# A gated linear attention followed by a two-layer network, on one core: second copy of v made by ScalarE in the first block, h copied out of PSUM by ScalarE for four turns, k' and the first states by VectorE, and the stages set at other slots

## The chip, the cores and the metric

The program runs on one core of a Trainium2 chip. The core has five engines that run their own instruction queues in order: TensorE (PE, with its weight loads shown apart as PEld), VectorE (DVE), ScalarE (ACT), GpSimd (POOL) and SyncE (SP), which here only issues DMA transfers. An engine that waits for another holds up everything behind the waiting instruction in its own queue. The metric is the device time of one execution in microseconds (us); lower is better.

## The reference

The first half is a recurrence over time for each of 4 x 8 heads of dimension 48, over 768 steps; the second half is a two-layer network on its output.

```python
f = 1.0 / (1.0 + np.exp(-f_logit))                       # q, k, v, f_logit: (4, 8, 768, 48)
for t in range(S):
    state = f[:, :, t, :, None] * state + np.einsum('bhd,bhe->bhde', k[:, :, t], v[:, :, t])
    y[:, :, t] = np.einsum('bhd,bhde->bhe', q[:, :, t], state)
x = y.transpose(0, 2, 1, 3).reshape(3072, 384)
h = x @ w_in                                             # (384, 2048)
sp = np.maximum(h, 0.0) + np.log1p(np.exp(-np.abs(h)))
out = (h * erf(sp)) @ w_out                              # (2048, 384)
```

All inputs and the output are float32, except that the weights come as 64-bit numbers, which the kernel rounds on the chip.

## The kernel before, in words

**Tiles.** Time is cut into 24 chunks g of 128 steps (six per batch entry), three chunks to a block of 384 rows; there are eight blocks. Within a chunk the decay is undone: q' is q times the cumulated decay, k' is k divided by it, so that the chunk's output is a masked product of scores and v, plus q' times the state that the chunks before have left.

**Stages of a chunk.** stage_d (L348): TensorE sums the logarithms of the decays (ps_d), ScalarE takes two exponentials (dp, kd), VectorE makes q' (qd, L372) and an engine makes k' (kd, L376): VectorE in block 0, GpSimd in all others. stage_t (L380): TensorE transposes both (ps_t), ScalarE copies q' out (qA, L395), ScalarE or VectorE copies k' out (kT, L397, L399). stage_s (L418): TensorE makes the state increments dS and the scores sc; VectorE masks the scores (L460) and next_state (L403) adds the increment to the old state (L415, VectorE) and multiplies by the chunk's total decay (L416, GpSimd). stage_y (L468): TensorE multiplies, in one go, masked scores and q' in qA with v and the state, which share the tile sv (L489), and ScalarE copies the result to xT (L493). From block 3 on stage_y of one chunk and stage_s of the next are one stage.

**The second copy of v.** A chunk's v is loaded twice: once as vt (for the state increments), and once, by load_sv (L222) in four 48 KB transfers, into sv beside the state. There are two sv tiles, which take turns. In each of the four transfers 64 steps of four heads go to one half of the partitions; these are rows that vt also holds, on the same or the other half.

**The network.** hidden (L544) makes h of a block in four groups of 512 columns. A group is two units u; a unit is six matmuls (L556) into a PSUM tile of two banks, which is then copied to the tile Hg: by ScalarE for blocks 0 and 1 (L566), by VectorE for the others (L568). There are two such PSUM tiles (ps_moe), which the output product (ops, L589, in project) also uses, so the unit after next waits for the copy. Each group is activated by `activate` (L503): a sigmoid (L156) into e, three tanh terms x (L159) that VectorE multiplies into e (L164), a last tanh (L524) and the product with h (L526). There are two e tiles, so the sigmoid of a group waits until L526 of the group before the last is done. A call of act_step moves the running groups on by one step each.

**The order.** The scheduler is off; instructions stand on their engines in the order in which the code issues them. First block 0's attention is written out (L705 to L744), with the loading and rounding of w_in between. Then the loop at L763 runs through turns `it`: turn it makes h of block it, the attention of block it + 1 and, from the third turn on (it = 2), the output of block it - 2. Each turn is a row of slots, one matmul of hidden or project each (96 in a full turn). At a slot may stand: a stage of attention (the list `at`, L770), an act_step (the rules at L788 to L797), loads, the preparation of the decays of block it + 2 (`prepare`, L330: a clamp on VectorE, Exp and Ln on ScalarE), and a step of weight rounding, which is one ScalarE and six VectorE instructions for each of 16 pieces of the weights (round_piece, L268).

**What ScalarE changes tables for.** Exp and Ln need one table, Sigmoid and Tanh another; each change is an ACT_TABLE_LOAD.

Of the kernel before, what the change touches and what calls it, by code (L numbers as in the profile page):

```python
# [45 lines left out]
ALU = mybir.AluOpType  # L46
# [27 lines left out]
def kernel(  # L74
# [10 lines left out]
    nc = tc.nc  # L85
    B, H, S, D = q.shape
# [8 lines left out]
    C = P // 2  # L95
    NCH = S // P
    CPB = 3
    TB = CPB * P
    n_blocks = B * S // TB
# [9 lines left out]
    def fixed(name, shape, dtype=FP32, pool=const):  # L109
        return pool.tile(shape, dtype, name=name)  # L110
# [14 lines left out]
    def rows(r, n=D):  # L125
        return slice(DP * r, DP * r + n)
# [53 lines left out]
    NV, NQ, NG = 3, 3, 10  # L180
    ADJACENT = 3
    vts = [fixed(f"vt{i}", [P, d_model], pool=fix) for i in range(NV)]

    NS, PAD = 2, DP - D
    svs = [fixed(f"sv{i}", [P, 2, 2, HP, D + 2 * PAD], pool=fix) for i in range(NS)]
# [33 lines left out]
    def half(c):  # L219
        return slice(C * c, C * (c + 1))  # L220

    def load_sv(g, queue=None):  # L222
        b, n = divmod(g, NCH)
        for r in range(2):
            for c in range(2):
                t0 = n * P + c * C
                (queue or nc.sync).dma_start(
                    out=svs[g % NS][half(1 - r), r, c, :, PAD : PAD + D],
                    in_=v[b, r::2, t0 : t0 + C, :].rearrange("a t d -> t a d"),
                )  # L230


    PIECE = 768
# [96 lines left out]
    def prepare(blk, j0, j1):  # L330

        lt = lts[blk][:, j0:j1, :].rearrange("t j c -> t (j c)")
        nc.vector.tensor_scalar(
            out=lt, in0=lt, scalar1=LOGIT_MIN, scalar2=None, op0=ALU.max
        )
        use_exp_ln()
        nc.scalar.activation(out=lt, in_=lt, func=AF.Exp, scale=-1.0)
        nc.scalar.activation(out=lt, in_=lt, func=AF.Ln, bias=1.0)
# [9 lines left out]
    def stage_d(g):  # L348
        blk, j = divmod(g, CPB)
        if blk == 0:  # L350
            both = ps_moe.tile([P, 2, 512], FP32, name="ps_d0", tag="moe")
            ps, totals[g] = both[:, 0, 0:d_model], both[:, 1, 0 : 2 * HP]
            busy.append(both[:, 1, P : 2 * P])
        else:
            ps = ps_at.tile([P, 512], FP32, name="ps_d", tag="at")[:, 0:d_model]
        nc.tensor.matmul(ps, lhsT=tri[:], rhs=lts[blk][:, j, :], start=True, stop=True)  # L356
        use_exp_ln()
        dp = dps[g % 2]
        kd = kds[g % 2][:, :, 0:D]
        nc.scalar.activation(  # L360
            out=dp[:, :, 0:D], in_=ps.rearrange("t (h d) -> t h d", d=D), func=AF.Exp, scale=-1.0
        )
        nc.scalar.activation(out=kd, in_=ps.rearrange("t (h d) -> t h d", d=D), func=AF.Exp)
        if blk > 0:
            for c in range(2):
                end = C * (c + 1)
                for a in range(HP):
                    nc.sync.dma_start(
                        out=Tall[:, g, c, a : a + 1],
                        in_=dp[end - 1 : end, 2 * a : 2 * a + 2, :].rearrange("o r d -> o (r d)"),  # L370
                    )
        nc.vector.tensor_tensor(  # L372
            out=qd[:, :, 0:D], in0=qns[g % NQ][:].rearrange("t (h d) -> t h d", d=D),
            in1=dp[:, :, 0:D], op=ALU.mult,
        )
        (nc.vector if blk == 0 else nc.gpsimd).tensor_tensor(  # L376
            out=kd, in0=kns[g % NQ][:].rearrange("t (h d) -> t h d", d=D), in1=kd, op=ALU.mult
        )

# [23 lines left out]
    def next_state(k, dS):  # L403

        g, c = divmod(k, 2)
        g1, c1 = divmod(k + 1, 2)
        for r in range(2):
            old = svs[g % NS][rows(r), r, c, :, PAD : PAD + D]
            new = svs[g1 % NS][rows(r), r, c1, :, PAD : PAD + D]
            total = Tall[rows(r), g, c, :].unsqueeze(2).broadcast_to((D, HP, D))  # L410
            add = dS[rows(r), c, :].rearrange("p (a d) -> p a d", a=HP)
            if k % (2 * NCH) == 0:
                nc.vector.tensor_tensor(out=new, in0=add, in1=total, op=ALU.mult)
                continue
            nc.vector.tensor_tensor(out=new, in0=add, in1=old, op=ALU.add)  # L415
            nc.gpsimd.tensor_tensor(out=new, in0=new, in1=total, op=ALU.mult)  # L416

    def stage_s(g):  # L418
        b, n = divmod(g, NCH)
# [124 lines left out]
    def hidden(blk, gi):  # L544

        own = n_made[0] % NG
        gr = {"h": Hgs[own], "done": False}
        n_made[0] += 1
        groups[blk, gi] = gr
        for u in range(FG // 2):  # L550
            hps = ps_moe.tile([P, 2, 512], FP32, name="hps", tag="moe")
            for j in range(2):
                ft = gi * FG + 2 * u + j
                assert ft * n_pieces // n_ft in rounded
                for kt in range(n_k):
                    nc.tensor.matmul(  # L556
                        hps[:, j, 0:TB],
                        lhsT=w_in_sb[:, kt, ft * P : (ft + 1) * P],
                        rhs=xTs[blk][:, kt, :],
                        start=(kt == 0), stop=(kt == n_k - 1),  # L560
                    )
                    if j == 1 and kt == n_k - 1:
                        assert all(i in rounded for i, x in enumerate(HOMES) if x == own)
                        to = gr["h"][:, 2 * u : 2 * u + 2, :]
                        if blk < 2:
                            nc.scalar.copy(out=to, in_=hps[:, :, 0:TB])  # L566
                        else:
                            nc.vector.tensor_copy(out=to, in_=hps[:, :, 0:TB])  # L568
                        if u == FG // 2 - 1:
                            acts.append(activate(gr))  # L570
                    yield
# [37 lines left out]
    def slots(it):  # L609

        if it >= n_blocks:
            return project(it - 2)
        made = [hidden(it, gi) for gi in range(n_g)]
        return chain(*made) if it < 2 else chain(*made[:2], project(it - 2), *made[2:])
# [20 lines left out]
    with tc.manual_schedule():  # L635
# [7 lines left out]
        load_f(1)  # L643
        load(1, "qk")
        load_f(2)
        load_sv(0)
        load_piece(0)
        load(1, "v")
        load(2)
        load_sv(1)  # L650
        load_piece(1)
        load_piece(2)
        for g in range(CPB, 2 * CPB):
# [3 lines left out]
            out=tri[:], in_=tri[:], pattern=[[1, P]], compare_op=ALU.is_ge, fill=0.0,  # L657
# [43 lines left out]
        def weights_steps(n):  # L701
            for _ in range(n):
                weights_step()
# [10 lines left out]
        load_piece(3)  # L714
        stage_d(1)
        prepare(0, 2, 3)
        stage_s(0)
        weights_steps(2)
        stage_t(1)
        load(4, "qk")  # L720
        load_piece(4)
        stage_d(2)
        weights_steps(2)
        stage_y(0)
        load_sv(2)
# [37 lines left out]
        for it in range(n_blocks + 2):  # L763
            blk = it + 1
            if it + 2 < n_blocks:
                for j in range(CPB):
                    load_f((it + 2) * CPB + j)
            todo = deque(stages(blk) if blk < n_blocks else [])
            n = n_slots[it]
            at = [int(3 + (n - 13) / max(1, len(todo)) * i) for i in range(len(todo))]  # L770
            for s, _ in enumerate(slots(it)):
                due += 1 if it == 0 and s < 36 else 0.75
                while due >= 1:
                    weights_step()
                    due -= 1
                if s % 6 == 3:
                    load_more()
                if at and s == at[0]:
                    at.pop(0)
                    f, g = todo.popleft()  # L780
                    f(g)
                    if f in (stage_y, stage_y_s):
                        if g + NS < n_chunks:
                            load_sv(g + NS)
                        load_to(g + LOOK)
                if it + 2 < n_blocks and s == (16 if it < 2 else 30):
                    prepare(it + 2, 0, CPB)
                if it == 0:  # L788
                    step = s >= 16 and s % 8 == 4
                elif it == 1:  # L790
                    step = s % 8 == 4
                elif it == 2:
                    step = s % 3 == 1
                elif it < n_blocks:
                    step = s % 7 in (2, 5)
                else:
                    step = s % 3 == 2  # L797
                if step and not 66 <= s < 72:
                    act_step()
                if it == n_blocks - 1 and s in (5, 40):  # L800
                    next(check)
            assert not todo
# [214 lines left out]
```

## Time and profile before

| | |
|---|---|
| time, median of 3 runs | 664.28 us (663.15 to 665.3) |
| span of the profiled execution | 663.1 us |
| TensorE busy | 618.4 us (93%) |
| VectorE busy | 454.3 us (69%) |
| ScalarE busy | 416.7 us (63%) |
| GpSimd busy | 92.1 us (14%) |
| mean TensorE clock granted | 0.965 |
| moved by DMA | 41.83 MB |

A line of the profile names a line of the program, an engine and an operation, then the tile written and the tiles read with their shape, how often, busy time, mean duration of one in ns, and after a bar the idle time of the engine just before it with the instruction that ended the idle time (the releaser). In a timeline the first two numbers are start and duration in us, and the brackets hold the idle time before. TensorE works on float32 in two passes, so that a matmul of the code is two instructions of the trace: a full unit of six matmuls is 12 of them. The end of a matmul is modelled, and a DMA counts as landed when its last part has.

### The profile page before, as it was taken

Reading aid. Unit: us, or ns where it says so; the run is one execution under the profiler, and the core shown is the slowest. Engines: PE = TensorE matmul, PEld = TensorE weight load, DVE = VectorE, ACT = ScalarE, POOL = GpSimd, SP = SyncE. Lnnn points to the kernel's source line nnn. Section 1 sums busy time; section 2 is a strip of 40 time slices with the busy share of each in tenths; the row PEclk is TensorE's granted clock in tenths of the full one; section 3 lists DMA queues with packets and bytes.
Section 4 is the critical chain, followed back from the end, with each engine's and each line's share of the span. In section 5 each row is a group of like instructions: output and inputs, shape, how many; then the busy total and the mean of one; then the engine's idle time right before and its main releaser. Section 6 shows DMA issues by size and latency. Waiting matters only on the chain.

```text
span 663.1 us, 11920 instructions
## 1 busy us (share of the span) xinstructions
PE 618.4 (93%) x4871; PEld 384.3 (58%) x4871; DVE 454.3 (69%) x525; ACT 416.7 (63%) x405; POOL 92.1 (14%) x120
## 2 busy tenths in 40 slices
PE   7749799796987999999999999999999999999996
PEld 6735466463554656666666656666666555555553
DVE  5667899989758387676767577676766578268450
ACT  5315775583796756696778866875657547266440
POOL 1212211221222001120112101120121100000000
PEclk9759999899799999999999999999999999999999
DMA  9796569342022141225022132032000100000101
GB/s 190 183 238 154 145 168 250 57 74 53 0 49 49 42 79 16 34 49 121 0 50 48 49 73 47 8 76 51 1 13 1 37 1 0 10 27 0 37 1 39
DMA packets 158909, 41.83 MB, mean 63 GB/s; under 512 B 150656, under 2 KB 153728, under 8 KB 158848
## 3 DMA queue, kind: packets, MB, share of 16 engines
q1 hardware_dynamic: 156768, 40.61, 28.4%
q8 instruction: 40, 0.66, 0.4%
q10 hardware_dynamic: 2080, 0.39, 0.3%
q14 instruction: 21, 0.17, 0.1%
HBM read 36.18 MB, written 4.72 MB: 62 GB/s over the span
## 4 chain that ended last, share of the span: by engine, by line
PE 72%; DVE 15%; issue 5%; DMA 3%; ACT 2%; SPq 1%; POOL 1%; DVEq 0%; ACTq 0%; POOLq 0%
PE ops L589 35%; PE hps L556 27%; DVE e L164 3%; PE y L489 3%; PE ps_t L388 2%; DVE qA L460 2%; PE ps_d L356 1%; DMA lt<-in_f_logit_dram 1%; PE sc L442 1%; PE sc L434 1%; DVE Hg L304 1%; DVE w_out_sb L295 1%; DVE sv L415 1%; DMA sv<-in_v_dram 1%; DVE w_out_sb L309 1%
## 5 line engine op out<-in xcount | busy, mean ns | idle before, releaser
L556 PE MATMUL hps<-xT,w_in_sb 128*128 128x384 f32 x768 | 266.6, 500 | 7.7 <-DVE Hg L568 7.1
L589 PE MATMUL ops<-w_out_sb,Hg 128*128 128x384 f32 x768 | 255.4, 489 | 3.4 <-DVE Hg L526 3.4
L556 PEld LDWEIGHTS hps<-xT,w_in_sb 128*128 128x128 f32 x768 | 146.4, 195 | 106.9 <-DVE Hg L568 8.3
L589 PEld LDWEIGHTS ops<-w_out_sb,Hg 128*128 128x128 f32 x768 | 145.0, 191 | 102.1 <-DVE Hg L526 4.0
L164 DVE SCALAR_TENSOR_TENSOR e<-x,e 128x1536 f32<-128x1536 f32 x96 | 172.8, 1800 | 17.3 <-ACT x L159 15.4
L159 ACT ACTIVATE x<-Hg,serf_bias 128x1536 f32<-128x1536 f32 x96 | 146.0, 1566 | 0.3
L156 ACT ACTIVATE e<-Hg,serf_bias 128x1536 f32<-128x1536 f32 x32 | 50.5, 1577 | 72.7 <-DVE Hg L526 72.6
L416 POOL TENSOR_TENSOR sv<-sv,Tall 48x192 f32<-48x192 f32 x80 | 54.1, 676 | 250.7 <-DVE sv L415 101.9
L568 DVE COPY Hg<-hps 128x768 f32<-128x768 f32 x48 | 45.7, 955 | 48.9 <-PE hps L556 48.5
L526 DVE TENSOR_TENSOR Hg<-Hg,e 128x1536 f32<-128x1536 f32 x32 | 56.9, 1778 | 19.5 <-ACT e L524 19.3
L460 DVE TENSOR_TENSOR qA<-sc,tri 64x256 f32<-64x256 f32 x96 | 40.5, 422 | 30.2 <-PE sc L442 28.5
L376 POOL TENSOR_TENSOR kd<-kn,kd 128x384 f32<-128x384 f32 x21 | 34.5, 1642 | 172.2 <-issue 132.3
L524 ACT ACTIVATE e<-e 128x1536 f32<-128x1536 f32 x32 | 47.2, 1475 | 3.6 <-DVE e L164 3.5
L372 DVE TENSOR_TENSOR qd<-qn,dp 128x384 f32<-128x384 f32 x24 | 15.8, 659 | 42.9 <-ACT dp L360 42.9
L489 PE MATMUL y<-qA,sv 128*32 128x64 f32 x1536 | 30.9, 232 | 14.2 <-DMA sv<-in_v_dram 6.6
L489 PEld LDWEIGHTS y<-qA,sv 128*32 128x32 f32 x1536 | 25.9, 117 | 27.3 <-issue 14.3
L360 ACT ACTIVATE dp<-ps_d 128x384 f32<-128x384 f32 x24 | 11.8, 491 | 36.5 <-PE ps_d L356 34.1
L395 ACT COPY qA<-ps_t 64x512 f32<-64x512 f32 x48 | 27.7, 576 | 10.2 <-PE ps_t L388 9.7
L493 ACT COPY xT<-y 128x384 f32<-128x384 f32 x24 | 11.5, 479 | 33.5 <-PE y L489 33.3
L415 DVE TENSOR_TENSOR sv<-sc,sv 48x192 f32<-48x192 f32 x80 | 28.4, 354 | 2.2
L596 ACT COPY osb<-ops 128x768 f32<-128x768 f32 x8 | 6.3, 787 | 33.4 <-PE ops L589 33.4
L156 ACT ACT_TABLE_LOAD x17 | 21.8, 1283 | 6.5 <-DVE Hg L526 6.2
(73 smaller groups left out, 383.8 us busy)
## 6 DMA issues: line engine op xcount, KB each, us to landing
lt<-in_f_logit_dram SPq DMA_DIRECT2D x24, 192.0 KB, 4.0
qn<-in_q_dram SPq DMA_DIRECT2D x24, 192.0 KB, 3.4
sv<-in_v_dram SPq DMA_DIRECT2D x96, 48.0 KB, 3.0
Hg<-in_moe_w_out_dram SPq DMA_DIRECT2D x6, 768.0 KB, 5.6
kn<-in_k_dram SPq DMA_DIRECT2D x23, 192.0 KB, 3.5
vt<-in_v_dram SPq DMA_DIRECT2D x23, 192.0 KB, 3.7
w_out_sb<-in_moe_w_in_dram SPq DMA_DIRECT2D x4, 768.0 KB, 5.7
Hg<-in_moe_w_in_dram SPq DMA_DIRECT2D x4, 768.0 KB, 6.8
```

The source lines that it names most:

```text
L156: nc.scalar.activation(out=dst[:], in_=h, func=AF.Sigmoid, bias=serf_bias[:, 0:1])
L159: nc.scalar.activation(out=dst[:], in_=h, func=AF.Tanh, bias=serf_bias[:, 1 + i : 2 + i], scale=SERF_KAB[i][0])
L164: nc.vector.scalar_tensor_tensor(out=e[:], in0=x[:], scalar=SERF_KAB[i][2], in1=e[:], op0=ALU.add, op1=ALU.mult)
L415: nc.vector.tensor_tensor(out=new, in0=add, in1=old, op=ALU.add)
L416: nc.gpsimd.tensor_tensor(out=new, in0=new, in1=total, op=ALU.mult)
L460: nc.vector.tensor_tensor(out=qA[half(1 - r), r, :, half(c)], in0=sc[half(c), r], in1=tri1[half(c)].unsqueeze(1).broadcast_to((C, HP, C)), ...
L489: nc.tensor.matmul(y[M * i : M * (i + 1), kt, half(c)], lhsT=sv[:, r, c, a, o : o + M], rhs=qA[:, r, a, half(c)], start=(n == 0), stop=Tru ...
L524: nc.scalar.activation(out=e[:], in_=e[:], func=AF.Tanh, scale=SERF_C)
L526: nc.vector.tensor_tensor(out=h, in0=h, in1=e[:], op=ALU.mult)
L556: nc.tensor.matmul(hps[:, j, 0:TB], lhsT=w_in_sb[:, kt, ft * P : (ft + 1) * P], rhs=xTs[blk][:, kt, :], start=(kt == 0), stop=(kt == n_k - 1),
L568: nc.vector.tensor_copy(out=to, in_=hps[:, :, 0:TB])
L589: nc.tensor.matmul(ops[tt // 2][:, tt % 2, 0:d_model], lhsT=gr["h"][:, j, tt * P : (tt + 1) * P], rhs=w_out_sb[:, ft, :], start=(ft == 0), ...
```

## The change

It has six parts. (1) In block 0 the second copy of v is no longer loaded: ScalarE copies it from vt. (2) In block 0 the multiplication by the total decay in next_state is done by VectorE and no longer by GpSimd. (3) h of blocks 2 and 3 is copied out of PSUM by ScalarE, as that of blocks 0 and 1 is already. (4) In the turn it = 2 act_steps are denser, and the decays of later blocks are prepared at slot 35 and no longer at 30 (from it = 2 on). (5) k' is made by GpSimd only for blocks 1 and 2, and by VectorE for the others. (6) From the turn it = 3 on, the stages of a chunk stand at slots 3, 16 and 23 of a third of the turn, where they were spread evenly. Parts 1 and 2 are for the start, in which DMA transfers and hops between engines set the pace; 3 and 5 move work between engines; 4 and 6 give the stages and activations other distances.

```diff
-    def load_sv(g, queue=None):
+    def load_sv(g):
         b, n = divmod(g, NCH)
         for r in range(2):
             for c in range(2):
+                to = svs[g % NS][half(1 - r), r, c, :, PAD : PAD + D]
+                if g < CPB:
+                    pairs = vts[g % NV][half(c)].rearrange("t (a r d) -> t a r d", r=2, d=D)
+                    nc.scalar.copy(out=to, in_=pairs[:, :, r, :])
+                    continue
                 t0 = n * P + c * C
-                (queue or nc.sync).dma_start(
-                    out=svs[g % NS][half(1 - r), r, c, :, PAD : PAD + D],
-                    in_=v[b, r::2, t0 : t0 + C, :].rearrange("a t d -> t a d"),
-                )
+                nc.sync.dma_start(out=to, in_=v[b, r::2, t0 : t0 + C, :].rearrange("a t d -> t a d"))
...
-        (nc.vector if blk == 0 else nc.gpsimd).tensor_tensor(
+        (nc.gpsimd if 0 < blk < ADJACENT else nc.vector).tensor_tensor(
             out=kd, in0=kns[g % NQ][:].rearrange("t (h d) -> t h d", d=D), in1=kd, op=ALU.mult
         )
...
             nc.vector.tensor_tensor(out=new, in0=add, in1=old, op=ALU.add)
-            nc.gpsimd.tensor_tensor(out=new, in0=new, in1=total, op=ALU.mult)
+            (nc.vector if g < CPB else nc.gpsimd).tensor_tensor(
+                out=new, in0=new, in1=total, op=ALU.mult
+            )
...
-                        if blk < 2:
+                        if blk < 4:
                             nc.scalar.copy(out=to, in_=hps[:, :, 0:TB])
...
-        load_sv(0)
         load_piece(0)
         load(1, "v")
         load(2)
-        load_sv(1)
...
         prepare(0, 2, 3)
+        load_sv(0)
         stage_s(0)
...
         stage_d(2)
+        load_sv(1)
...
-            at = [int(3 + (n - 13) / max(1, len(todo)) * i) for i in range(len(todo))]
+            if it >= n_blocks - 1 or blk <= ADJACENT:
+                at = [int(3 + (n - 13) / max(1, len(todo)) * i) for i in range(len(todo))]
+            else:
+                at = [3 + n // CPB * j + k for j in range(CPB) for k in (0, 13, 20)][: len(todo)]
...
-                if it + 2 < n_blocks and s == (16 if it < 2 else 30):
+                if it + 2 < n_blocks and s == (16 if it < 2 else 35):
                     prepare(it + 2, 0, CPB)
...
                 elif it == 2:
-                    step = s % 3 == 1
+                    step = s % 5 in (1, 3)
```

ADJACENT is 3, CPB (chunks per block) is 3, n_blocks is 8.

## The prediction

> **What bounds the kernel now.** I read the busy times by stage first, because the shares on the page are means over stages with different limits. Columns: stretch, its length, busy time of TensorE (PE), weight loads, VectorE (DVE), ScalarE (ACT), GpSimd (POOL), then TensorE's granted clock, the DMA share and GB/s.
>
> ```profile
> 0.00:55.00 55.00, 37.82 (x524) 30.43 (x525) 33.51 (x68) 21.94 (x37) 11.07 (x24) 0.78 0.93 208
> 55.00:130.00 75.00, 65.83 (x800) 40.88 (x802) 69.37 (x103) 46.55 (x62) 17.35 (x23) 0.97 0.63 152
> 130.00:166.00 36.00, 30.31 (x294) 18.29 (x285) 32.80 (x45) 23.08 (x25) 6.89 (x8) 0.93 0.34 62
> 166.00:240.00 74.00, 66.46 (x553) 40.35 (x554) 46.25 (x52) 54.19 (x50) 12.47 (x13) 0.93 0.25 48
> 305.00:520.00 215.00, 215.00 (x1700) 132.78 (x1702) 152.41 (x162) 150.19 (x136) 33.80 (x40) 1.00 0.22 41
> ```
>
> Four regimes. To 55 us the DMA engines are full (share 0.93) and nothing else is. From 55 to 166 VectorE is the limit: 69.37 + 32.80 of 111 us. From 166 to 240 no engine is full and TensorE idles 7.5 us. From 240 on TensorE never stops: 215.00 of 215. So only what stands before 240 can be won; what comes later can only be lost.
>
> Next the waits by pair (total, times, longest), for what ends TensorE's gaps, then the timeline for when they fall.
>
> ```profile
> ACT e L156 <- DVE Hg L526: 72.6, 20, 9.4
> PE hps L556 <- DVE Hg L568: 7.1, 2, 6.3
> PE y L489 <- DMA sv<-in_v_dram: 6.6, 1, 6.6
> PE ps_t L388 <- POOL kd L376: 3.5, 3, 1.9
> PE ops L589 <- DVE Hg L526: 3.4, 1, 3.4
> ```
>
> ```profile
> 42.43 2.48 PE L489 MATMUL y<-qA,sv 128*32 128x64 f32 x64 [6.64 <-DMA sv<-in_v_dram]
> 166.66 8.42 PE L556 MATMUL hps<-xT,w_in_sb 128*128 128x384 f32 x16 [6.35 <-DVE Hg L568]
> 214.24 2.93 PE L589 MATMUL ops<-w_out_sb,Hg 128*128 128x384 f32 x4 [3.44 <-DVE Hg L526]
> ```
>
> The third y of block 0 waits for the second copy of v, and everything after it follows. At 160.3 TensorE waits until VectorE, behind its backlog, copies h out of PSUM. At 210.8 it waits for the activation of block 0's last group.
>
> The prices, by line: engine, shape, count, busy us, mean ns.
>
> ```profile
> L568 DVE COPY Hg<-hps 128x768 f32<-128x768 f32 x48 | 45.7, 955 | 48.9 <-PE hps L556 48.5
> L566 ACT COPY Hg<-hps 128x768 f32<-128x768 f32 x16 | 12.7, 794 | 7.9 <-PE hps L556 7.4 <-ACT kd L363 0.5
> L376 DVE TENSOR_TENSOR kd<-kn,kd 128x384 f32<-128x384 f32 x3 | 2.0, 653 | 0.0
> L415 DVE TENSOR_TENSOR sv<-sc,sv 48x192 f32<-48x192 f32 x80 | 28.4, 354 | 2.2
> ```
>
> **What the Trainium skill says.** "SBUF — State Buffer", Who interferes with whom: a VectorE instruction with two SBUF inputs and a GpSimd instruction that reads SBUF exclude each other for a whole instruction. The trace agrees: k' takes 0.995 to 2.617 us on GpSimd and 0.55 us in two of three cases on VectorE, and beside GpSimd's 161.5 to 164.0 us VectorE's multiply of e takes 2.06 us instead of 1.75. "TensorE: Matmul & The Clock Gate", What's actually happening: after an idle window of some 3.4 us the clock is halved. The trace agrees: granted clock 0.50 from 30 to 50 us, and 8 passes of hps take 5.00 us there against 2.58 (0.3225 each) later; the 8.42 us above for 16 passes is 3.3 over. "ScalarE: Activation LUTs", What ACT_TABLE_LOAD costs: 186 ns plus 0.833 ns per element; for a 192-element copy that is an estimate of 0.35 us. The trace has none from SBUF; from its 768- and 384-element copies (0.794 and 0.479 us) 192 elements come to 0.32. I take 0.35.
>
> **Part 1, the copies of v.** Twelve 48 KB loads go, 0.59 MB: at the 208 GB/s of this stage 2.8 us of transfer, and 2.78 + 4.01 + 2.65 us of SyncE's issue time. Twelve ScalarE copies come, 12 x 0.35 = 4.2 us, in three fours of 1.3 us. The first four stand ahead of a weight piece and chunk 1's qA copies and delay them by at most 0.8 us; the other eight fall into ScalarE's idle time at 18 to 25 us (2.94 and 3.19 us).
>
> **Part 2, the first states.** Ten multiplies of 0.676 us on GpSimd (L416) become ten of 0.355 on VectorE: 3.6 us more for an engine with 21.5 us free before 55, and two engine hops fewer in each state.
>
> **Parts 1 and 2 together: when does y(2) start?** VectorE gets to chunk 2's masks (L460) at 34.12, after standing 2.57 us for block 1's f_logit at 32.06 (L333). Those loads come at least 0.39 MB / 208 GB/s = 1.9 us earlier, but six of the new multiplies, 2.1 us, and the 0.8 us of above lie ahead: masks again at about 34.3, to 36.1. Two adds and two multiplies, 1.4 us: states ready at 37.5, so y(2) starts near 37.8 instead of 42.43, 4.6 us sooner. VectorE then ends its weight piece at about 43.0 (before 41.54) but no longer stands 4.72 us, to 46.25, for the next one: 3.2 us sooner there, and 4.6 at the next wait, the q' of chunk 3 at 51.68, which hangs on TensorE. From 52 to 160 VectorE has a fixed list of work, so the shift stays. **I take 4.5 us**; bounds 2.5 (another load, or the new multiplies, end the wait) and 6.6 (all of it).
>
> **Part 3, h of blocks 2 and 3 by ScalarE.** Sixteen copies leave VectorE (15.3 us) and cost ScalarE 16 x 0.794 = 12.7. In the changed order of ScalarE the first copy of block 2 stands ahead of the sigmoid that waits 9.40 us for VectorE's L526, the second behind that sigmoid and one tanh. So the first unit is copied at about 157, TensorE goes on through the third unit (3.9 us) at 160.3 and stops near 164 until the second copy at 167.6: a wait of 3.6 instead of 6.35.
>
> **Part 4, denser steps in block 2's turn** (29 steps of 72 slots instead of 24) and the preparation moved from slot 30 to 35, beside a stage that uses the same table. From the sigmoid at 163.67 to the tanh that ends at 209.15 ScalarE worked 40.6 us and waited 4.9. With three table loads fewer (3.8), three h copies more (2.4) and an xT copy that now comes later (0.5) it is 38.6. Walking both orders side by side with these durations, the tanh ends near 205, its multiply near 207, and TensorE gets to that group at 210.5 without a wait: 3.7 us sooner, 1.6 more because the four passes after the wait (2.93 us) run at full clock, 0.8 for the wait at 239.8. That is 6.1; on the way there are two new waits of some 2 us (ops for the third unit's copy at 176, y(10) for the qA copy at 204), counted in it. Whether the wait at 164 still halves the clock is open (up to 2 us): **I take 5**; bounds 0 and 10.
>
> **Part 5, k' of blocks 3 to 7 by VectorE.** 15 x 0.6 = 9 us on VectorE, 15 x 1.64 = 24.6 off GpSimd. One falls in the full stretch (0.55 us, partly in a wait of 2.14 at 135.6). Later VectorE has 63 us free in 215. k' is ready about 1 us sooner; of the TensorE waits for it (3.5 us) some 2.5 go, counted in part 4's walk.
>
> **Part 6, stages placed anew from block 3's turn on.** From k' to transposes 13 slots instead of some 9, from transposes to y only 7: 4.5 us instead of 6. y needs the PSUM buffer that the qA copy frees; that copy ended between 1.2 and 7 us after its transposes before. Nothing can be won here; a few y will wait. In block 3's turn ScalarE also has eight h copies, whose delay holds hps back: walking that order I find waits of 1.4, 0.3 and 0.2 us in its first third. **I take +2 for that turn and +0.5 for the later ones**; bounds 0 and 6.
>
> **Sum.** 664.3 - 4.5 - 5 + 2.5 = 657.3, say 657.
>
> **Rivals.**
> (a) ScalarE becomes the bound in the turns of blocks 2 and 3: its tanh and h copies wait on VectorE in one queue. For it: 54.19 of 74 us busy and the 72.6 us of sigmoid waits; against: 2 us less work in the stage. Part 4 then gives nothing: 664.3 - 4.5 + 2.5 = 662.3.
> (b) Slower: TensorE, full after 240, gets small waits at most of the twelve y of four turns (0.7 us each, 8.4), hps waits in block 3's turn (3), and only the head (4.5) is won: 671, or 667 with half of them. For it: the copy that took 7 us; against: no wait at all in 15 such distances before.
> (c) Full effect: the head gives 6.4 and the stretch to 240 gives 9 with the clock kept: 649.
> (d) The second copy of v is hidden anyway: against it speaks the 6.64 us gap, the longest of TensorE's. I give it no share apart from the bound of 2.5.
>
> **How the numbers follow.** Forecast 0.60, (a) 0.17, (b) 0.09, (c) 0.14. The best case of all bounds is 664.3 - 16.6 = 648, the worst 664.3 - 2.5 + 6 = 668; a range of 650 to 663 leaves out about a tenth on each side. 0.3% is 2 us, so the border is at 662.3: half of (a) counts as the same. Faster 0.60 + 0.14 + 0.09 = 0.83, same 0.08, slower 0.09.
>
> **What would show it.** Step 1: y(2) starts at 37 to 39 us with no DMA behind it. Step 2: at 130 us the same instructions stand some 4.5 us earlier. Step 3: the wait of hps for Hg near 160 is 3 to 4 us and ends on ScalarE. Step 4: the wait of ops for L526 is gone and TensorE is about 10 us ahead at the end of block 2's turn. Step 5: k' on VectorE near 0.6 us. Step 6: TensorE idle between 240 and 520 is 1 to 4 us. The prediction is wrong if y(2) waits for another load, or if hps or y wait on ScalarE copies again and again after 230.

## The result, and the profile after

The changed kernel takes 655.34 us (median of 4 runs, 653.53 to 656.07) where the kernel before, on the same chip, takes 664.79 (663.15 to 665.3). The ratio is 0.9858, with a 95% interval of 0.9829 to 0.9887, so some 9 us are won. The forecast was 657.0.

Line numbers are now 3 to 5 higher (L415 and L416 are L418 and L419, L489 is L494, L568 is L573). First the busy times by stage, in the columns and stretches used before.

```profile
0.00:55.00 55.00, 43.15 (x599) 33.55 (x600) 39.44 (x83) 28.23 (x52) 5.04 (x15) 0.84 0.93 220
130.00:166.00 36.00, 32.02 (x290) 19.39 (x289) 30.66 (x43) 24.17 (x27) 4.62 (x6) 1.00 0.30 55
166.00:240.00 74.00, 69.54 (x563) 42.45 (x562) 50.59 (x54) 64.77 (x61) 7.34 (x10) 0.95 0.26 49
305.00:520.00 215.00, 213.64 (x1703) 132.30 (x1702) 149.54 (x162) 154.01 (x139) 25.06 (x32) 1.00 0.21 41
```

TensorE is busier wherever it idled before (43.15 for 37.82 us at the start, 69.54 for 66.46 from 166 to 240). ScalarE goes from 54.19 to 64.77 us in that third stretch, GpSimd from 12.47 to 7.34. After 305 us TensorE is no longer quite full.

The waits by pair that answer to those shown before:

```profile
PE hps L561 <- ACT Hg L571: 3.1, 1, 3.1
PE y L494 <- POOL sv L419: 3.1, 3, 1.4
PE sc L439 <- DVE sv L418: 2.5, 1, 2.5
PE ops L594 <- ACT Hg L571: 2.4, 1, 2.4
```

Of the three long waits of before, y's for the DMA (6.6) and that of ops for L526 (3.4) are gone; that of hps for h (6.3) is halved and ends on ScalarE. New is the wait of ops for ScalarE's copy of h. The wait of sc for VectorE's state addition has grown from 0.95 to 2.5 us; it is that of the third chunk's state increments, which are made in the tile sc. The timeline shows when they fall.

```profile
37.57 1.42 PE L494 MATMUL y<-qA,sv 128*32 128x64 f32 x36
39.34 1.07 PE L494 MATMUL y<-qA,sv 128*32 128x64 f32 x28 [0.35 <-DVE sv L419]
162.38 1.56 PE L561 MATMUL hps<-xT,w_in_sb 128*128 128x384 f32 x4 [3.14 <-ACT Hg L571]
350.42 1.21 PE L494 MATMUL y<-qA,sv 128*32 128x64 f32 x64 [1.36 <-POOL sv L419]
```

y(2) starts at 37.57 instead of 42.43. A wait like the last stands at 275.75 too (1.40); these two are the only ones over 0.3 us after 240. The releaser in the brackets is inferred by the profile, and for these two it will turn out to be another one.

**A ruler.** Three sections of TensorE's timeline tell the parts apart: **a**, to the start of the first hps (y(2) stands just ahead of it); **b**, from there to the start of the y of chunk 11, the last of block 3 (it ends in the turn it=2); **c**, from there to the start of the last unbroken run of output products, which takes 62.08 us in every kernel. Here are all kernels that ran, with the device time and its ratio to the kernel before, and the three sections from the profiled execution.

| kernel | median us | ratio (95%) | a | b | c |
|---|---|---|---|---|---|
| before | 664.79 | | 45.48 | 183.49 | 366.94 |
| changed | 655.34 | 0.9858 (0.9829 to 0.9887) | 40.98 | 178.10 | 368.85 |
| e1_head: parts 1, 2 only | 660.39 | 0.9936 (0.9917 to 0.9955) | 41.31 | 183.31 | 366.93 |
| e2_copies: part 1 only | 657.81 | 0.9910 (0.9895 to 0.9924) | 38.46 | 183.36 | 366.94 |
| e3_states: part 2 only | 664.47 | 1.0008 (1.0001 to 1.0014) | 43.59 | 183.46 | 366.93 |
| e4_noh: without part 3 | 655.84 | 0.9868 (0.9849 to 0.9887) | 41.10 | 178.61 | 368.85 |
| e5_nosteps: without part 4 | 661.70 | 0.9970 (0.9959 to 0.9981) | 39.04 | 181.82 | 372.07 |
| e6_nok: without part 5 | 654.23 | 0.9858 (0.9840 to 0.9876) | 40.70 | 177.96 | 367.56 |
| e7_even: without part 6 | 654.70 | 0.9863 (0.9846 to 0.9881) | 39.14 | 178.61 | 368.25 |
| e10_nostates: without part 2 | 654.56 | 0.9851 (0.9837 to 0.9866) | 40.05 | 178.97 | 368.81 |
| e11_prep30: slot 30 again | 654.98 | 0.9876 (0.9857 to 0.9896) | 39.24 | 176.75 | 369.13 |
| e12_early: state step earlier | 653.69 | 0.9851 (0.9832 to 0.9870) | 39.16 | 178.58 | 367.81 |
| e13_clock: idle TensorE filled | 653.66 | 0.9858 (0.9836 to 0.9881) | 37.42 | 178.63 | 368.88 |
| e14_best: four edits together | 655.60 | 0.9863 (0.9843 to 0.9884) | 37.39 | 181.66 | 368.18 |

How fine the ruler is, kernels with equal code in a section tell. c agrees within 0.01 us in the four with the old turns (366.93 to 366.94) and within 0.07 in the changed kernel, e10 and e13 (368.81 to 368.88); b within 0.18 in the first four, within 0.9 in the changed kernel, e7, e10 and e13 (178.10 to 178.97); a only within 2.3 (39.04 to 41.31 in the eight profiles with both parts 1 and 2).

So the changed kernel gains 4.50 us in a (5.4 on the mean of those eight profiles, 40.08) and 5.39 in b, and gives 1.91 back in c; the sum is 7.98 of the 8.7 us between the spans of the two profiles. The gain in a is known to some 2 us only: the kernel before has one profile, and e3, which is no faster, has an a 1.89 us shorter. The kernel before was timed anew beside each group of runs (medians 663.79 to 664.79), and each ratio is to those of its own group.

### The profile page after: what moved, and what is told of

It is laid out like the page before. It is cut to its first block, busy times and chain, and to the rows that moved or that the text cites. A ratio compares the mean times of both kernels' runs of the same rounds, so it can differ in the third digit from the quotient of the medians.

```text
span 654.4 us, 11941 instructions
## 1 busy us (share of the span) xinstructions
PE 617.7 (94%) x4871; PEld 384.6 (59%) x4871; DVE 445.4 (68%) x534; ACT 431.9 (66%) x432; POOL 66.9 (10%) x95
## 4 chain that ended last, share of the span: by engine, by line
PE 70%; DVE 16%; ACT 6%; issue 4%; SPq 1%; DMA 1%; POOL 0%; ACTq 0%; DVEq 0%; POOLq 0%
PE ops L594 33%; PE hps L561 27%; DVE e L164 3%; PE y L494 3%; PE ps_t L391 2%; DVE qA L465 2%; DVE sv L418 2%; SPq L371 1%; PE ps_d L359 1%; PE sc L439 1%; PE sc L447 1%; DVE Hg L307 1%; DVE w_out_sb L298 1%; ACT x L159 1%; DVE Hg L302 1%
## 5 line engine op out<-in xcount | busy, mean ns | idle before, releaser
L561 PE MATMUL hps<-xT,w_in_sb 128*128 128x384 f32 x768 | 262.1, 494 | 3.7 <-ACT Hg L571 3.1
L419 POOL TENSOR_TENSOR sv<-sv,Tall 48x192 f32<-48x192 f32 x70 | 54.9, 784 | 364.3 <-issue 213.9
L573 DVE COPY Hg<-hps 128x768 f32<-128x768 f32 x32 | 30.5, 955 | 34.2 <-PE hps L561 34.1
L375 DVE TENSOR_TENSOR qd<-qn,dp 128x384 f32<-128x384 f32 x24 | 14.2, 591 | 48.6 <-ACT dp L363 48.6
L494 PE MATMUL y<-qA,sv 128*32 128x64 f32 x1536 | 31.5, 233 | 9.9 <-ACT qA L398 5.4
L494 PEld LDWEIGHTS y<-qA,sv 128*32 128x32 f32 x1536 | 26.1, 117 | 23.3 <-ACT qA L398 7.7
L571 ACT COPY Hg<-hps 128x768 f32<-128x768 f32 x32 | 25.3, 792 | 13.7 <-PE hps L561 10.2
L418 DVE TENSOR_TENSOR sv<-sc,sv 48x192 f32<-48x192 f32 x80 | 28.4, 355 | 2.3
L340 ACT ACTIVATE lt<-lt 128x1152 f32<-128x1152 f32 (+1 forms) x10 | 9.7, 974 | 26.3 <-DVE lt L336 26.3
```

Source lines behind the costliest of these rows:

```text
L419: (nc.vector if g < CPB else nc.gpsimd).tensor_tensor(out=new, in0=new, in1=total, op=ALU.mult)
L494: nc.tensor.matmul(y[M * i : M * (i + 1), kt, half(c)], lhsT=sv[:, r, c, a, o : o + M], rhs=qA[:, r, a, half(c)], start=(n == 0), stop=Tru ...
L561: nc.tensor.matmul(hps[:, j, 0:TB], lhsT=w_in_sb[:, kt, ft * P : (ft + 1) * P], rhs=xTs[blk][:, kt, :], start=(kt == 0), stop=(kt == n_k - 1),
```

## Experiments

**Which part of the head's edits does it?** e1_head is the changed kernel with parts 3 to 6 undone, e2_copies has part 1 alone, e3_states part 2 alone.

```diff
 # e2_copies and e10_nostates, against a kernel with both parts
-            (nc.vector if g < CPB else nc.gpsimd).tensor_tensor(
+            nc.gpsimd.tensor_tensor(
 # e3_states, with load_sv(0) and load_sv(1) back among the first loads
-                if g < CPB:
+                if False:
```

> Parts 1 and 2 alone (copies of v by ScalarE in block 0, first states on VectorE), the other four parts undone. My theory: the head's gain and that of the later parts add up, so y(2) starts near 37.6 us as in the changed kernel, everything to 160 us stands 4.9 us earlier, the waits of 6.35 us near 156 and of 3.44 us near 205 are both there as before, and the time is 664.8 - 4.9 = 659.9, ratio 0.993. Rival: the turn it=2 hangs on the chain of ScalarE's and VectorE's activations, which does not move with the head; then the wait at 205 grows and the time stays at 663 to 665, ratio 1.000.

> Part 1 alone: copies of v by ScalarE, first states still multiplied by GpSimd. My theory: the loads ended the wait, so most of the gain is here; the first half of y(2) starts near 37.6 us, its second half waits for GpSimd's last multiply near 40.7 us where VectorE's came at 39.3: 1.4 us less gain, so 664.8 - 3.5 = 661.3, ratio 0.995. Rival: part 2 was needed, since the states come late from GpSimd: y(2) starts past 40.7 and the gain is below 2 us, ratio 0.998 or more.

> Part 2 alone: first states on VectorE, v still loaded twice. My theory: y(2) still waits for the DMA of sv to 42 us, no gain: 664 to 665, ratio 0.999 to 1.001. Rival: the states, not the loads, were the limit: 660 to 662, ratio 0.995.

e1 measured 0.9936: the head's 4.2 us of 664 stay to the end, since b and c are those of before; the waits of 6.36 and 3.43 us are both there, only earlier. The rival (the time stays) is refuted. e3 gains nothing: y(2) still waits for the DMA.

```profile
40.59 2.44 PE L494 MATMUL y<-qA,sv 128*32 128x64 f32 x64 [7.08 <-DMA sv<-in_v_dram]
```

e2 was the miss: part 1 alone wins more than both parts (0.9910 beside 0.9936, run together). The state increments of the third chunk (L439; the expectations call them scores, after the tile sc in which they are made) and the second half of its y, first with both parts (e1), then with part 1 alone (e2):

```profile
32.49 0.89 PE L439 MATMUL sc<-vt,kd 64*48 64x48 f32 x32 [2.50 <-DVE sv L418]
39.66 1.07 PE L494 MATMUL y<-qA,sv 128*32 128x64 f32 x28 [0.35 <-DVE sv L419]
```

```profile
30.35 0.57 PE L439 MATMUL sc<-vt,kd 64*48 64x48 f32 x32 [0.95 <-DVE sv L418]
36.81 1.07 PE L494 MATMUL y<-qA,sv 128*32 128x64 f32 x28 [0.76 <-POOL sv L419]
```

They overwrite the increments of the chunk before, which VectorE's L418 reads, and with part 2 the multiplies stand ahead of L418 in VectorE's queue (three of 0.35 us from one chunk's masks to the last of these additions): the wait is 2.50 instead of 0.95 us. On the other side the state multiply on GpSimd makes y wait 0.76. Then e10_nostates took part 2 out of the whole change.

> The changed kernel without part 2: first states multiplied by GpSimd again. With part 1 alone the head was 2.8 us shorter than with parts 1 and 2. My theory: VectorE, in order, is the limit of the head once the loads are gone, and each multiply on it delays what the next scores wait for; y(2) starts at 34.4 us and its second half at 36.8 us, and the 2.5 to 2.8 us stay to the end: 655.3 - 2.6 = 652.7, ratio 0.982. Rival: the later turns, tuned to the other start, give it back: 655 to 656.

Its ratio, 0.9851, is that of the changed kernel, as the rival had it, and a is 40.05. The 2.6 us between e1 and e2 are not all part 2's. The durations above show the rest: the same increments took 0.89 us in e1 and 0.57 in e2. That is TensorE's clock. Four profiles with both parts (e5, e7, e11, e12) ran them in 0.57 to 0.58 us as e2 did, and their second half of y(2) starts at 37.40 to 37.59; e2's at 36.81. **At equal clock part 2 costs some 0.7 us of a**, and gains nothing there. The runs' times, too, put most of the 2.6 us down to the clock: two of e1's six runs had a mean granted clock of 0.973 and 0.976 and took 658.43 and 657.12 us, within 0.2 us of e2's range (0.973 to 0.976, 656.96 to 658.24); the other four, at 0.968 and 0.969, took 659.91 to 661.27.

**Is it the clock that moves the head by 2 us?** e13_clock fills two idle stretches of TensorE with products that nobody reads.

```diff
+        keep_busy(11, -2)   # ahead of stage_y(0), into the tile of the chunk before
         stage_y(0)
...
+        keep_busy(8)        # ahead of stage_s(2)
         stage_s(2)
```

> The changed kernel with 19 more dummy matmuls in two of TensorE's idle stretches of the head (11 after the third ps_d near 16 us, 8 ahead of the third chunk's scores near 30 us), which take no other work's place. Kernels with the same head differ by 2 us in where y(2) ends (37.4 to 39.7), and those with the later end show a clock of 0.5 from 32 to 36 us. My theory: TensorE's idle stretches let its clock fall, and where they fall against the work makes the 2 us: with the fill the clock is 1.0 from 20 to 36 us, y(2)'s second half starts at 37.4 or before, and the time is 655.3 - 1.5 = 653.8, the spread smaller. Rival: the head's end is set by loads and by VectorE, and the clock only goes with it: no change, 655 to 656.

TensorE alone in two stretches, for the changed kernel and then for e13: stretch, length, busy time, granted clock, DMA share, GB/s.

```profile
28.00:32.00 4.00, 1.18 (x56) 0.89 1.11 274
32.00:36.00 4.00, 3.58 (x73) 0.50 1.05 287
```

```profile
28.00:32.00 4.00, 3.48 (x86) 1.00 1.00 249
32.00:36.00 4.00, 2.29 (x46) 1.00 1.07 291
```

With the fill the clock is 1.00 from 12 to 36 us, y(2)'s second half starts at 36.21, 3.1 us before the changed kernel's, and a is 37.42 (37.39 in e14, which has the same fill), below all eight profiles without it. So idle stretches do set the clock there, and the clock the length of a. In the time it shows less: 653.66 us, but a ratio equal to the changed kernel's, and a spread of runs that is no smaller (652.43 to 655.34). The low clock came later instead (0.67 from 36 to 40). Whether anything stays to the end is open.

**Which part makes b?** e4_noh, e5_nosteps and e11_prep30 undo part 3, part 4, and the second half of part 4.

```diff
-                        if blk < 4:                     # e4_noh
+                        if blk < 2:
-                    step = s % 5 in (1, 3)              # e5_nosteps
+                    step = s % 3 == 1
-                if it + 2 < n_blocks and s == (16 if it < 2 else 35):   # e5_nosteps, e11_prep30
+                if it + 2 < n_blocks and s == (16 if it < 2 else 30):
```

> The changed kernel without part 3: h of blocks 2 and 3 is copied by VectorE again. My theory: the wait of hps near 156 us grows back from 3.1 to about 6 us on VectorE, and VectorE has 15 us more in a stretch that hangs on it, so that the activations of the turn it=2 come later: 655.3 + 3 = 658.5, ratio to before 0.990. Rival: the 12.7 us that ScalarE is freed of make up for it in the stretch to 240 us: 655 to 656, ratio 0.986.

> The changed kernel without part 4: act_steps in the turn it=2 at every third slot again, preparation at slot 30. My theory: the steps' rate sets when block 0's last group is activated, so the wait of ops for L531 of 3 us or more near 205 is back and the stretch to 240 loses 4 to 6 us: 655.3 + 5 = 660.3, ratio 0.9935. Rival: parts 3 and 5, which relieve VectorE, have made the activations fast enough: the wait is under 1 us and the time 655 to 657.

> The changed kernel with only the preparation of the decays moved back from slot 35 to slot 30 (from the turn it=2 on); the denser act_steps stay. All of part 4 undone cost 6.4 us. My theory: the density of the steps is the larger half, since they set when the last group of block 0 is done; slot 30 costs the table loads, about 1.3 us each where ScalarE is full, so 655.3 + 1.5 = 656.8. Rival: the slot is the larger half (it separates Exp and Ln from the tanh of the same stretch in six turns): 659 or more.

In e4 the wait near 160 comes back as expected, and yet b grows by 0.5 only, c not at all, and the time is the changed kernel's: the rival was right.

```profile
161.70 8.43 PE L561 MATMUL hps<-xT,w_in_sb 128*128 128x384 f32 x16 [6.22 <-DVE Hg L573]
```

Of the 3.1 us that part 3 saves there it pays 2.43 at the next product, where ops waits for ScalarE's copy of h and then runs its eight passes at half clock (4.54 us; 2.85 in e5 and e11):

```profile
170.98 4.54 PE L594 MATMUL ops<-w_out_sb,Hg 128*128 128x384 f32 x8 [2.43 <-ACT Hg L571]
```

The wait moved from one engine's queue to another's. e4 has none there.

e5 is the expected large loss, 0.9970. Its waits in the turn it=2, and one in the turn after:

```profile
190.87 3.49 PE L594 MATMUL ops<-w_out_sb,Hg 128*128 128x384 f32 x10 [1.25 <-DVE Hg L531]
204.51 2.93 PE L594 MATMUL ops<-w_out_sb,Hg 128*128 128x384 f32 x4 [3.43 <-DVE Hg L531]
281.45 0.57 PE L439 MATMUL sc<-vt,kd 64*48 64x48 f32 x32 [1.92 <-DVE sv L418]
```

The products wait for block 0's activation again. e5 and e11 differ in the density of the steps alone: b 181.82 against 176.75, c 372.07 against 369.13. **The denser steps are worth 5.1 us in b and 2.9 in c, 8.0 together** (the two ratios differ by 0.0094, which is 6.2 us); without them parts 3, 5 and 6 would have ended 3.5 us behind the kernel before (b + c: 553.89 against 550.43). The move to slot 35 is worth nothing: with slot 30 b is 1.35 shorter and c 0.28 longer, and the time is the same. I had expected slot 30 to cost 1.5. It does bring three table loads more from 166 to 240 us (11 of 1.283 us instead of 8), but b is no longer for them.

**Which part gives back in c?** e6_nok returns k' of blocks 3 to 7 to GpSimd, e7_even spreads the stages evenly again, e12_early issues the second state step of a chunk ahead of stage_d of the next.

```diff
-        (nc.gpsimd if 0 < blk < ADJACENT else nc.vector).tensor_tensor(   # e6_nok
+        (nc.vector if blk == 0 else nc.gpsimd).tensor_tensor(
-            if it >= n_blocks - 1 or blk <= ADJACENT:                     # e7_even
+            if True:
+        late.pop(g - 1, int)() if blk >= ADJACENT else None               # e12_early, in stage_d
```

> The changed kernel without part 5: k' of blocks 3 to 7 by GpSimd again. My theory: k' comes about 1 us later, which matters only where its transposes follow closely, that is in the turn it=2 (blocks 3); later 13 slots lie between: 655.3 + 1.5 = 656.8. Rival 1: GpSimd's multiply was what slowed VectorE's (2.06 instead of 1.75 us beside it), and its return costs in every turn: 658 or more. Rival 2: VectorE's 9 us were missed elsewhere: 654 or less.

> The changed kernel without part 6: stages spread evenly over the turns from it=3 on. My theory: the two waits of 1.4 us of y for GpSimd's state multiply, at 275.8 and 350.4, come from the 7 slots between transposes and y, in which the late state stands behind two 1.8 us multiplies on VectorE; with the even spread they are gone and no other comes: 655.3 - 2.8 = 652.5, ratio 0.9815. Rival: closer k' and transposes bring waits of their own (1 to 3 us): 654 to 657.

> The changed kernel, but from block 3 on the second state step of a chunk is issued 13 slots earlier, at stage_d and not at stage_t of the next chunk. My theory: the waits of y for GpSimd's state multiply at 275.8 and 350.4 come from the state's addition standing behind two 1.8 us multiplies on VectorE when only 7 slots are left to y; issued earlier, both waits are gone and TensorE's end moves by 2.5: 652.8, ratio 0.982. Rival: y waits next for the qA copy, which is queued behind the same activations (0.8 us of each 1.4 stay, as it was with k' by GpSimd): 654.5.

None of the three differs from the changed kernel in time, so the numbers I wrote for e6 (a loss), e7 (2.8 us won) and e12 (2.5 won) were wrong. In c, where the ruler is fine, e6 is 1.29 shorter, e7 0.60 and e12 1.04. e6 and e7 come to 1.89 of the 1.91 given back, but that such gains add up is not shown (e14 below speaks against it). In e7 both waits of y are gone, as I had expected, but two waits of hps come in their place (0.90 at 287.97, 1.02 at 449.39).

Two of these expectations put the waits of y down to GpSimd's state multiply, as the profile names it. The code and the trace say otherwise. At that place the multiply makes the state of the *next* chunk, in the other sv tile, which this y does not read. What y does need is a PSUM tile: y takes turns with the transposes ps_t in the two tiles of the pool ps_at, so a copy out of one of them has to be done first. The changed kernel, at both waits:

```profile
270.53 3.62 DVE L164 SCALAR_TENSOR_TENSOR e<-x,e 128x1536 f32<-128x1536 f32 x2 [5.30 <-ACT x L159]
274.18 0.74 DVE L418 TENSOR_TENSOR sv<-sc,sv 48x192 f32<-48x192 f32 x2
274.96 0.69 DVE L402 COPY kT<-ps_t 128x512 f32<-128x512 f32 x1
275.75 1.21 PE L494 MATMUL y<-qA,sv 128*32 128x64 f32 x64 [1.40 <-POOL sv L419]
```

```profile
349.16 1.16 ACT L398 COPY qA<-ps_t 64x512 f32<-64x512 f32 x2
349.83 1.08 POOL L419 TENSOR_TENSOR sv<-sv,Tall 48x192 f32<-48x192 f32 x2 [18.34 <-issue]
```

The copy of k' ends at 275.65 and y starts at 275.75; the copies of q' end at 350.32 and y starts at 350.42, while GpSimd's second multiply runs on to 350.91. In e6 the profile itself names these two copies:

```profile
274.79 1.10 PE L494 MATMUL y<-qA,sv 128*32 128x64 f32 x64 [0.86 <-DVE kT L402]
348.82 1.10 PE L494 MATMUL y<-qA,sv 128*32 128x64 f32 x64 [0.84 <-ACT qA L398]
```

So VectorE stands 5.30 us for a tanh, two multiplies of e and the state's additions run, and only then the copy that y waits for; at 350 ScalarE's copies stand behind a sigmoid. e12 takes the additions (0.74 us) out from ahead of VectorE's copy, and the first wait falls by 0.78 to 0.62. The second falls to 1.07. For it the profile names no releaser, but again a copy of k' ends 0.10 us ahead of y:

```profile
347.25 0.69 DVE L403 COPY kT<-ps_t 128x512 f32<-128x512 f32 x1
348.04 1.18 PE L495 MATMUL y<-qA,sv 128*32 128x64 f32 x63 [1.07 <-issue]
```

What part 5 has to do with it is seen further up the same chain. On VectorE k' stands ahead of the clamp of the decays (L336), which ScalarE's Exp waits for, and behind Exp stand Ln, a table load and the tanh above. First the changed kernel, then e6:

```profile
264.01 0.55 DVE L379 TENSOR_TENSOR kd<-kn,kd 128x384 f32<-128x384 f32 x1
265.26 1.17 ACT L340 ACTIVATE lt<-lt 128x1152 f32<-128x1152 f32 x1 [1.38 <-DVE lt L336]
```

```profile
264.35 1.16 ACT L340 ACTIVATE lt<-lt 128x1152 f32<-128x1152 f32 x1 [0.91 <-DVE lt L336]
```

Exp waits 0.47 us less in e6, and 0.48 less in the next turn (0.91 for 1.39). The two waits of y are 0.54 and 0.52 less, 1.06 of the 1.29.

**Do the small gains add up?** e14_best takes e13's fill, slot 30, k' by GpSimd and e12's state step together.

> The changed kernel with the fill of the head (19 dummy matmuls), the preparation at slot 30, k' of blocks 3 to 7 by GpSimd and the second state step issued at stage_d: the four edits whose traces were ahead of the changed kernel's, together. Counted from the first hps to the last output products, the changed kernel takes 546.95 us, with slot 30 545.88, with k' by GpSimd 545.52, with the early state 546.39; the fill brings the first hps from 39.0 to 41.3 us forward to 37.4. My theory: these add up, 37.4 + 546.95 - 1.1 - 1.4 - 0.6 = 581.3 for the start of the last output products, 6.6 before the changed kernel's 587.93, and with the head's spread of 2 us in mind a time of 650 to 651, ratio 0.979. Rival: they win the same slack of VectorE and ScalarE and only the largest counts: 652 to 653.5, ratio 0.983.

They don't: 655.60 us. a is 37.39 and c 0.67 shorter than the changed kernel's, but b is 3.56 longer, with waits that none of the four edits has alone in this size:

```profile
164.62 0.66 PE L392 MATMUL ps_t<-ident,kd 128*128 128x128 f32 x4 [1.87 <-POOL kd L380]
189.68 1.11 PE L392 MATMUL ps_t<-ident,qd 128*128 128x128 f32 x4 [3.72 <-DVE qd L376]
```

In c too there is a wait that none of them has alone, 1.63 us of ps_t for k' on GpSimd at 344.12. So the sum of that expectation fails, and its rival, which still had the largest gain stay, fails too. No version here is faster than the changed kernel by more than the intervals.

## Why the prediction was right, step by step

**The sum holds section by section.** Head 4.5 forecast, 4.50 in a; turn it=2 5 forecast, 5.39 in b; later +2.5 forecast, +1.91 in c. Cut where the forecast cuts, at the first hps of block 3 (243.74 before, 232.81 after), the last two are 6.43 and +2.95, still near 5 and 2.5; TensorE is 10.9 us ahead there, about 10 forecast. That a agrees to 0.1 us is luck, since the same code spreads over 2.3. What stands behind the numbers is in part not what I argued.

**Part 1** is the whole of the head's gain (e2, e3), and a copy takes 348 to 353 ns, the 0.35 us of the estimate. That the first four delay chunk 1's work by at most 0.8 us was too small: y(0) starts at 20.89 instead of 19.18, since it stands behind a wait for an exponential that ScalarE reaches after those copies (3.77 us, before 2.78). At y(1) 0.70 of it is left (27.65, before 26.95).

**Part 2** I counted as two hops fewer. Its step failed: VectorE is the engine the state increments wait for, and at equal clock the part costs 0.7 us of a. The bound of 6.6 us on the head was also too low: part 1 alone brought 7.0 in a (e2), of which up to 2 may be the clock's. The walk to y(2) met its number by two errors that cancel. VectorE reaches the third chunk's masks at 35.97, not 34.3, because it then stands 1.41 us for TensorE, at half clock (35.77); the last states are ready at 39.3, not 37.5. But y(2) does not need them to start: its first 36 products run while VectorE makes them, so that y(2) starts at 37.57, and ends at 40.4 where the walk would have it.

**Part 3**: the wait of 3.6 us was forecast, 3.14 measured, ending on ScalarE as foreseen. Its worth is 0.5 us in b, less than the ruler's error there. In this rival (a), ScalarE in place of VectorE, was half right.

**Part 4**: the wait for L526 is gone and one of the two new waits came as walked (2.43 us of ops for the third unit's copy, ending at 171, which is the forecast 176 less the head's gain); in place of the other, y(10) for the qA copy, the transposes waited 2.03 us for q'. The three table loads fewer that I put into the sum play no part (e11). The density alone counts, and it counts for 8.0, since without it the later turns lose too. (Of the first 72 slots 26 have a step, before 22, not 29 and 24: slots 66 to 71 never have one.) The last tanh of block 0 ends at 201.0 and its multiply at 202.8, as walked less the head's gain. Whether a wait would still halve the clock was left open: it does, from 171.0 and from 191.5 for 3.4 us each, where the kernel before has 10.2 us from 162.5 and 3.4 from 213.7.

**Part 5** runs at 0.552 us, forecast 0.6. "One falls in the full stretch" was the only cost I saw. It costs 1.29 us in c (e6), and 1.06 of them are its place ahead of the clamp in VectorE's queue, and so of Exp, tanh and the copies that y waits for. **Part 6** costs 0.60, not 2.5. Its mechanism, that y waits for the PSUM tile which the copy of q' frees, was right for one of the two waits; at the other it is the copy of k'. The waits for ScalarE's copies of h in block 3's turn did not come. TensorE's idle time from 240 to 520, 2.8 us, is within the 1 to 4 forecast.

**Rivals.** (b), slower, needed waits at most of twelve y; there were two. (c), full effect, needed 9 us in the stretch to 240 with the clock kept; it gave 6.4, and the clock fell to half twice. (d) fell with e3 and e2: the second copy of v was what y(2) waited for.

## What to carry to other kernels

A change of six parts can live on two of them: undo each part alone, and measure sections whose code is equal, and how far these agree: in c 0.1 us shows, in a not even 2. When work is taken from one in-order queue and put into another, look for what stands behind it there before counting a hop saved. The releaser that a profile names is an inference; check that the waiting instruction really reads, or overwrites, what that releaser handles. A rule that paces calls, such as the steps here, can be worth more than moving work between engines.

## What was not expected of the hardware

With the same code up to there, the first hps started anywhere between 39.04 and 41.31 us, with a granted clock of 0.50 to 0.70 from 32 to 36 us and the same products at 0.57 or 0.89 us. The eight profiles fall into two groups. In four the clock stands at half for 13.7 us there (31.1 to 44.8 in the changed kernel), and a is 40.70 to 41.31; in the other four for 10.2 us, and a is 39.04 to 39.24. The stretches at half clock in all these traces, but for the last one of each, last 3.4 us or a multiple of it. So the groups differ by one such stretch, in which TensorE does 1.7 us less work (an estimate: half of 3.4). The Trainium skill, "TensorE: Matmul & The Clock Gate", What's actually happening, says that the window in which the clock's activity is judged is free-running, so that the same kernel meets it at another phase in each run. The runs agree: where the half clock falls against the work differs from run to run, and a fill of the idle stretches took it out of 12 to 36 us.
